# An attention stage beside a mixture layer on one core: q's transposes as fp32r from DMA copies, and the stages from the transposes on one slot later

## The chip, the cores and the metric

The kernel runs on one core of a Trainium2 chip. The metric is the device time of one execution in microseconds, the median of several runs. Engines are called as in the profile: PE (TensorE), DVE (VectorE), ACT (ScalarE), POOL (GpSimd) and SP (SyncE, which here only issues DMAs).

## What is computed

Three parts follow one another. The first is a linear attention with a complex decay per channel; the reference steps through the 768 positions of each of 4 x 8 heads of width 48:

```python
for t in range(S):
    ar, ai = (a_re_n[:, :, t, :, None], a_im_n[:, :, t, :, None])
    new_re = ar * S_re - ai * S_im
    new_im = ar * S_im + ai * S_re
    kv = np.einsum('bhd,bhe->bhde', k[:, :, t], v[:, :, t])
    S_re, S_im = (new_re + kv, new_im)
    y[:, :, t] = np.einsum('bhd,bhde->bhe', q[:, :, t], S_re)
```

Its result, 3072 tokens of 384, goes through `g = h * tanh(softplus(h))` with `h = x @ w_in` (384 to 2048) and `g @ w_out`, called the first layer here, and then through `(a * b) @ w_out` with `a = x @ w_a`, `b = x @ w_b` (384 to 1536), the second layer.

## The kernel before, in words

**Chunks.** The attention is cut into 24 chunks: six stretches of 128 positions for each of 4 batch entries, all 8 heads together. Chunk c belongs to stretch c // 4. In a chunk the decay's logarithm and its angle are summed along the positions by a product with a triangle matrix (`sum_ell`, `sum_theta`, line 329), exponentials and sines of the sums scale and rotate q and k (`scale_qk`, `trig`, `rotate`), and from there it is an ordinary masked attention with a running state: q and k are transposed on PE (line 410), four heads in one PSUM bank, so two banks for q and two for k; ACT copies them to SBUF (`qT`, `kT`); `scores` multiplies them (line 433) and DVE keeps the lower triangle in `am` (line 439); `values` adds the product of q with the state W and of the scores with v (line 463); `outer` and `state` bring W up to date (lines 502 and 515). `store_y` and `store_y2` split the result into a rounded part `yh` (ACT) and a rest `yl` (DVE), each in a tile of its own of which there is one, store both to DRAM, and `read_x` loads them as columns of the first layer's input `xh`, `xl`.

**Units.** The first layer works in 6 blocks of 512 tokens, one for each stretch, and 16 units of 128 hidden columns each. A unit is nine matmuls `hps` (line 594), a chain on DVE and ACT that ends in the product `m` (lines 600 to 614), its two parts `gh` and `gl` (lines 620, 621), and, two units later on PE, nine matmuls `x2ps` (line 637). In block 0 the product is not split, and `x2ps` takes three matmuls of plain float32. The second layer (lines 692 and 717) follows alone.

**Slots.** The first four chunks are worked before the first unit, in an order written out by hand. The other 20 run beside blocks 0 to 4, the four chunks of stretch j+1 beside block j. A table gives each step of a chunk a slot; chunks follow at 8 slots, and 32 slots go over a block's 16 units:

```python
early = [
    (-4, load_a), (0, decay_1), ..., (7, sum_theta), (6, decay_exp), (8, reduce_angle),
    (8, hand_turn), (7, hand_end), (7, scale_qk), (11, trig),
]
late = [
    (10, read_end), (11, load_v), (14, lambda c: transposes(c, 0)), (15, lambda c: transposes(c, 1)),
    (16, lambda c: scores(c, 0)), (16, lambda c: scores(c, 1)), (17, values), (17, outer),
    (17, state), (18, store_y), (19, store_y2), (20, read_x),
]
```

`load_qk` stands in slot 4 and `rotate` in slot 12. Where a block begins in slots is taken from the last entry of `late` (`ready_slot`, `ends`). A scheduler then sets the order on each engine from the written order, its own estimate of when things are ready, and the buffers: q, k, `qhp` (rotated q, in the tile QH) and `khp` have one buffer each, PSUM tiles of the tag `ps` three, and `hps` two. All DMAs of this part are issued by SP, in their order.

Of the kernel before, what the change touches and what calls it, by code (L numbers as in the profile page):

```python
# [10 lines left out]
F32 = mybir.dt.float32  # L11
F32R = mybir.dt.float32r
# [9 lines left out]
def kernel(  # L22
# [14 lines left out]
    nc = tc.nc  # L37
# [26 lines left out]
    B, H, S, D = q.shape  # L64
# [3 lines left out]
    P = 128  # L68
    C = 128
# [6 lines left out]
    HH = H // 2  # L76
# [13 lines left out]
    const = ctx.enter_context(tc.tile_pool(name="const", bufs=1))  # L90
    dram = ctx.enter_context(tc.tile_pool(name="dram", bufs=1, space=DRAM))

    ident = const.tile([P, P], F32, name="ident")
    csum = const.tile([P, P], F32, name="csum")
    csum_r = const.tile([P, P], F32R, name="csum_r")
    tsum = const.tile([P, P], F32, name="tsum")
    good_i = const.tile([1, 1], I32, name="good_i")
    bias_one = const.tile([P, 1], F32, name="bias_one")
# [27 lines left out]
    ap1 = att.enter_context(tc.tile_pool(name="ap1", bufs=1, side="right"))  # L126
# [5 lines left out]
    qT = [ap1.tile([P, HH, C], F32, name=f"qT{i}") for i in range(2)]  # L132
    W = [ap1.tile([P, H * D + PAD], F32, name=f"W{b}") for b in range(B)]
    QH, KH = (ap1.tile([P, 2 * H, 64], F32, name=nm) for nm in ("qhp", "khp"))
# [124 lines left out]
    def in_rows(c, nm):  # L259

        if c < B:
            return pair(c, nm, nm, "h", "a")
        own = QH if nm == "qh" else KH
        if nm == "qh":
            nc.gpsimd.memset(own[:, :, D:], 0.0)
        st[nm, c] = own.rearrange("p (h a) d -> p h a d", a=2)[..., :D]
        return st[nm, c]
# [124 lines left out]
    def rotate_one(c, nm, eng):  # L392
        w = st["turn", c].rearrange("p a h d -> p h a d")
        x = st.pop((nm, c)).rearrange("p h (o d) -> p h o d", o=1).to_broadcast([P, H, 2, D])
        eng.tensor_tensor(in_rows(c, nm + "h"), x, w, ALU.mult)

    def rotate(c):
        rotate_one(c, "q", nc.vector)
        rotate_one(c, "k", nc.vector)

    def transposed(c, nm, hf):

        src = st[nm[0] + "h", c]
        pool, tag = (ps_h, "h") if c < B and nm == "kT" else (ps_a, "ps")
        K = D2 if c < B else P
        p = pool.tile([P, HH, C], F32, tag=tag, name="p" + nm)[:K]
        own = (QH if nm == "qT" else KH).rearrange("p (h a) d -> p h (a d)", a=2)
        for i in range(HH):
            h = hf * HH + i
            nc.tensor.transpose(p[:, i, :], src[:, h].rearrange("p a d -> p (a d)") if c < B else own[:, h], ident)  # L410
        st["p" + nm, c, hf] = p

    def transposed_out(c, nm, hf):
        K = D2 if c < B else P
        if c % 2 and c < B:
            t = ap0.tile([P, HH, C], F32, tag=f"{nm}{hf}", name=nm)[:K]
        else:
            t = (qT[hf] if nm == "qT" else ap2.tile([P, HH, C], F32, tag=nm, name=nm))[:K]
        st[nm, c, hf] = t
        act(out=t, in_=st.pop(("p" + nm, c, hf)), func=AF.Copy)  # L420

    def transposes(c, hf):
        for nm in ("qT", "kT"):
            transposed(c, nm, hf)
            transposed_out(c, nm, hf)
# [4 lines left out]
    def scored_in(c, hf):  # L430
        p = st["psc", c, hf] = ps_a.tile([P, HH, C], F32, tag="ps", name="psc")
        for i in range(HH):
            nc.tensor.matmul(  # L433
                p[:, i, :], lhsT=st["kT", c, hf][:, i, :], rhs=st["qT", c, hf][:, i, :], start=True, stop=True
            )

    def scored_out(c, hf):
        causal = csum.bitcast(I32).rearrange("p (o c) -> p o c", o=1).to_broadcast([P, HH, C])
        nc.vector.copy_predicated(scored(c)[hf], causal, st.pop(("psc", c, hf)))

    def scores(c, hf):
        scored_in(c, hf)
        scored_out(c, hf)
# [103 lines left out]
    def slot_0(c):  # L547
# [3 lines left out]
    early = [  # L551
        (-4, load_a), (0, decay_1), (1, decay_2), (1, decay_3), (2, tangent), (2, decay_4), (3, angle),
        (3, split_ell),
        (4, carry), (4, split_theta), (5, sum_ell), (7, sum_theta), (6, decay_exp), (8, reduce_angle),
        (8, hand_turn), (7, hand_end), (7, scale_qk), (11, trig),
    ]
    late = [
        (10, read_end), (11, load_v), (14, lambda c: transposes(c, 0)), (15, lambda c: transposes(c, 1)),
        (16, lambda c: scores(c, 0)), (16, lambda c: scores(c, 1)), (17, values), (17, outer),
        (17, state), (18, store_y), (19, store_y2), (20, read_x),  # L560
    ]
    plan = {}
    for c in range(B, NCH):
        for n, (r, fn) in enumerate(early + late + [(4, load_qk), (12, rotate)]):
            plan.setdefault(slot_0(c) + r, []).append((-r, c, n, fn))
# [183 lines left out]
    def judge(pool):  # L749
# [20 lines left out]
        out=csum, in_=csum, pattern=[[1, P]], compare_op=ALU.is_ge, fill=0.0, base=0, channel_multiplier=-1  # L770
    )
    make_identity(nc, ident)
    nc.vector.tensor_copy(csum_r, csum)
    nc.vector.tensor_scalar(tsum, csum, 1.0 / TWO_PI, None, ALU.mult)
    for t in am + am0 + W + qT + [KH]:
        nc.gpsimd.memset(t, 0.0)
# [136 lines left out]
    for ui in range(len(units) + lag):  # L913
        if ui == 3:
            behind(after_lead, last)
        if ui < len(units):
# [6 lines left out]
            p = moe1_h(blk, f, ps_a if blk == NB - 1 and f % 2 else ps_h)  # L923
# [232 lines left out]
```

## Time and profile before

| | us |
|---|---|
| median of 3 runs | 1092.7 (1091.62 to 1093.75) |
| the profiled execution | 1092.23 |
| its span, first to last instruction | 1090.4 |
| PE busy | 1048.8 |
| DVE busy | 653.7 |
| ACT busy | 611.5 |
| POOL busy | 232.0 |

A busy time is the union of an engine's instructions. Matmuls overlap: one starts before the last has drained, so their mean durations add up to more than PE's busy time, and the spacing of two starts, not the duration, says what one costs in a full stream. In a row of a timeline "x4" merges four instructions of one kind; the time in it runs from the first start to the last end. Brackets at the end of a row hold the idle time before it and what ended it.

### The profile page before, as it was taken

Reading aid. Unit: us, or ns where it says so; the run is one execution under the profiler, and the core shown is the slowest. Engines: PE = TensorE matmul, PEld = TensorE weight load, DVE = VectorE, ACT = ScalarE, POOL = GpSimd, SP = SyncE. Lnnn points to the kernel's source line nnn. Section 1 sums busy time; section 2 is a strip of 40 time slices with the busy share of each in tenths; the row PEclk is TensorE's granted clock in tenths of the full one; section 3 lists DMA queues with packets and bytes.
Section 4 is the critical chain, followed back from the end, with each engine's and each line's share of the span. In section 5 each row is a group of like instructions: output and inputs, shape, how many; then the busy total and the mean of one; then the engine's idle time right before and its main releaser. Section 6 shows DMA issues by size and latency. Waiting matters only on the chain.

```text
span 1090.4 us, 15921 instructions
## 1 busy us (share of the span) xinstructions
PE 1048.8 (96%) x6060; PEld 874.0 (80%) x6060; DVE 653.7 (60%) x998; ACT 611.5 (56%) x968; POOL 232.0 (21%) x265
## 2 busy tenths in 40 slices
PE   4989999999999999999999999999999999999997
PEld 1856666788888888888877778888888888888886
DVE  6799966787677777777579998532322322422222
ACT  8868877898788887798767742221221222212211
POOL 2012343444334344333231123100000000000000
PEclk9989999999999999999999999999999999999999
DMA  9557752344434343433155366110100100100000
GB/s 206 107 153 191 173 152 66 67 96 87 111 80 82 67 95 80 87 97 80 30 164 183 124 217 212 43 58 1 30 29 1 58 1 1 44 1 1 29 1 32
DMA packets 203550, 90.92 MB, mean 83 GB/s; under 512 B 144782, under 2 KB 187851, under 8 KB 203467
## 3 DMA queue, kind: packets, MB, share of 16 engines
q1 hardware_dynamic: 202410, 89.62, 32.9%
q8 instruction: 50, 0.82, 0.3%
q10 hardware_dynamic: 1056, 0.21, 0.1%
q14 instruction: 34, 0.27, 0.1%
HBM read 72.44 MB, written 17.36 MB: 82 GB/s over the span
## 4 chain that ended last, share of the span: by engine, by line
PE 70%; DVE 13%; ACT 6%; issue 5%; DMA 3%; POOL 2%; SPq 1%; ACTq 0%; DVEq 0%; POOLq 0%
PE ops L717 12%; PE psb L692 12%; PE psa L692 12%; PE x2ps L637 12%; PE hps L594 11%; PE psc L433 3%; PE py L463 3%; ACT m L59 3%; PE pkT L410 2%; DVE wf L168 1%; PE pqT L410 1%; ACT L54 1%; DVE wf L169 1%; DVE m L600 1%; DVE wf L167 1%
## 5 line engine op out<-in xcount | busy, mean ns | idle before, releaser
L703 DVE TENSOR_TENSOR a_sb<-a_sb,psb 128x512 f32<-128x512 f32 x72 | 49.4, 686 | 224.9 <-PE psb L692 224.9
L59 ACT ACTIVATE m<-m 128x512 f32<-128x512 f32 x192 | 119.5, 632 | 68.8 <-DVE m L600 64.0
L59 ACT ACTIVATE a_sb<-psa 128x512 f32<-128x512 f32 x72 | 43.0, 597 | 163.6 <-PE psa L692 161.6
L59 ACT ACTIVATE ph<-a_sb 128x512 fp32r<-128x512 f32 x72 | 45.4, 631 | 155.5 <-DVE a_sb L703 155.5
L594 PE MATMUL hps<-xh,winh 128*128 128x512 f32 x288 | 119.1, 415 | 4.7 <-DVE gh L611 3.3
L621 POOL TENSOR_TENSOR gl<-m,gh 128x512 fp32r<-128x512 f32 x64 | 83.2, 1300 | 151.9 <-DVE gh L620 131.6
L594 PE MATMUL hps<-xh,winl 128*128 128x512 f32 x288 | 114.2, 396 | 0.0
L594 PE MATMUL hps<-xl,winh 128*128 128x512 f32 x288 | 114.1, 396 | 0.0
L717 PE MATMUL ops<-woh,ph 128*128 128x384 f32 x288 | 97.1, 337 | 0.0
L717 PE MATMUL ops<-woh,pl 128*128 128x384 f32 x288 | 97.1, 337 | 0.0
L717 PE MATMUL ops<-wol,ph 128*128 128x384 f32 x288 | 96.7, 336 | 0.0
L637 PE MATMUL x2ps<-gl,wouth 128*128 128x512 f32 x240 | 94.3, 393 | 2.4 <-DVE gl L621 1.4
L637 PE MATMUL x2ps<-gh,wouth 128*128 128x512 f32 x240 | 94.1, 405 | 1.8 <-ACT gh L59 1.5
L637 PE MATMUL x2ps<-gh,woutl 128*128 128x512 f32 x240 | 94.0, 392 | 0.0
L614 DVE SCALAR_TENSOR_TENSOR m<-m,hps 128x512 f32<-128x512 f32 x80 | 54.6, 684 | 63.1 <-ACT m L59 62.6
L692 PE MATMUL psa<-xh,wal 128*128 128x512 f32 x216 | 85.2, 394 | 0.0
L692 PE MATMUL psa<-xl,wah 128*128 128x512 f32 x216 | 85.1, 394 | 0.0
L692 PE MATMUL psa<-xh,wah 128*128 128x512 f32 x216 | 84.4, 391 | 0.3 <-DVE a_sb L703 0.3
L692 PE MATMUL psb<-xh,wbh 128*128 128x512 f32 x216 | 84.2, 390 | 0.0
L692 PE MATMUL psb<-xh,wbl 128*128 128x512 f32 x216 | 84.2, 390 | 0.0
L692 PE MATMUL psb<-xl,wbh 128*128 128x512 f32 x216 | 84.2, 390 | 0.0
L705 DVE TENSOR_TENSOR pl<-a_sb,ph 128x512 fp32r<-128x512 f32 x72 | 52.2, 726 | 39.0 <-ACT ph L59 39.0
(167 smaller groups left out, 2332.1 us busy)
## 6 DMA issues: line engine op xcount, KB each, us to landing
wraw<-in_moe_w_out_dram SPq DMA_DIRECT2D x14, 768.0 KB
wraw<-in_moe_w_in_dram SPq DMA_DIRECT2D x8, 768.0 KB
a<-in_a_re_dram SPq DMA_DIRECT2D x24, 192.0 KB
q<-in_q_dram SPq DMA_DIRECT2D x24, 192.0 KB
k<-in_k_dram SPq DMA_DIRECT2D x24, 192.0 KB
v<-in_v_dram SPq DMA_DIRECT2D x24, 192.0 KB
wraw<-in_moe_w_a_dram SPq DMA_DIRECT2D x6, 768.0 KB
wraw<-in_moe_w_b_dram SPq DMA_DIRECT2D x6, 768.0 KB
```

What stands on the lines that cost most here:

```text
L59: x = nc.scalar.activation(**kw)
L410: nc.tensor.transpose(p[:, i, :], src[:, h].rearrange("p a d -> p (a d)") if c < B else own[:, h], ident)
L433: nc.tensor.matmul(p[:, i, :], lhsT=st["kT", c, hf][:, i, :], rhs=st["qT", c, hf][:, i, :], start=True, stop=True)
L463: nc.tensor.matmul(p[par * 64:(par + 1) * 64, i, :], lhsT=w[:, col:col + 64], rhs=x[:, first + par, :], start=(n == 0), stop=(n == len(ter ...
L594: nc.tensor.matmul(p, lhsT=w[:, kk, :], rhs=x[:, kk, :], start=(i == 0), stop=(i == len(ops) - 1))
L614: nc.vector.scalar_tensor_tensor(m, m, 2.5, p, ALU.subtract, ALU.mult)
L621: (nc.vector if on_act else nc.gpsimd).tensor_tensor(gl, m, gh.bitcast(F32), ALU.subtract)
L637: nc.tensor.matmul(x2ps[m], lhsT=w[:, ms], rhs=x, start=(f == 0 and i == 0), stop=(f == NF - 1 and i == len(terms) - 1),)
L692: nc.tensor.matmul(p, lhsT=w[:, kk, :], rhs=x[:, kk, :], start=(i == 0), stop=(i == len(ops) - 1))
L703: nc.vector.tensor_tensor(a_sb, a_sb, pb, ALU.mult)
L705: nc.vector.tensor_tensor(lo, a_sb, hi.bitcast(F32), ALU.subtract)
L717: nc.tensor.matmul(ops_t[t], lhsT=x[:, tsl], rhs=w, start=(f == 0 and i == 0), stop=(f == NF2 - 1 and i == 2),)
```

## The change

q's transposes of the 20 later chunks take their operand from a copy of rotated q that two DMAs of 128 x 512 float32 (256 KB) write right behind the rotation, one for each half of the heads. The copies are typed fp32r, as are the identity and the view of PSUM that is written; bits are moved, none is rounded. The copies lie in the tiles `yh` and `yl`, taken under the same tags, so that a copy can be written once the previous chunk's result has been stored from there. k's transposes stay float32. In the table the transposes and all that follows stand one slot later, except `outer`, which stays in slot 17 and now stands ahead of `values`. `sum_theta`, `reduce_angle` and `hand_turn` stand one slot earlier. Blocks begin one slot later in slot numbers, so the later steps keep their distance to the units and the earlier ones come a slot sooner.

```diff
+    ident_r = const.tile([P, P], F32R, name="ident_r")
...
+    QR = []
+
     def rotate(c):
         rotate_one(c, "q", nc.vector)
+        QR[:] = [ap1.tile([P, HH, C], F32R, tag=nm, name="qr") for nm in ("yh", "yl")]
+        for hf in range(2):
+            nc.sync.dma_start(
+                out=QR[hf].bitcast(F32), in_=QH[:, hf * H:(hf + 1) * H].rearrange("p (h a) d -> p h (a d)", a=2)
+            )
         rotate_one(c, "k", nc.vector)
...
             h = hf * HH + i
+            if c >= B and nm == "qT":
+                nc.tensor.transpose(p[:, i, :].bitcast(F32R), QR[hf][:, i], ident_r)
+                continue
             nc.tensor.transpose(p[:, i, :], src[:, h].rearrange("p a d -> p (a d)") if c < B else own[:, h], ident)
...
-        (4, carry), (4, split_theta), (5, sum_ell), (7, sum_theta), (6, decay_exp), (8, reduce_angle),
-        (8, hand_turn), (7, hand_end), (7, scale_qk), (11, trig),
+        (4, carry), (4, split_theta), (5, sum_ell), (6, sum_theta), (6, decay_exp), (7, reduce_angle),
+        (7, hand_turn), (7, hand_end), (7, scale_qk), (11, trig),
     ]
     late = [
-        (10, read_end), (11, load_v), (14, lambda c: transposes(c, 0)), (15, lambda c: transposes(c, 1)),
-        (16, lambda c: scores(c, 0)), (16, lambda c: scores(c, 1)), (17, values), (17, outer),
-        (17, state), (18, store_y), (19, store_y2), (20, read_x),
+        (10, read_end), (11, load_v), (15, lambda c: transposes(c, 0)), (16, lambda c: transposes(c, 1)),
+        (17, lambda c: scores(c, 0)), (17, lambda c: scores(c, 1)), (17, outer), (18, values),
+        (18, state), (19, store_y), (20, store_y2), (21, read_x),
     ]
...
+    nc.vector.tensor_copy(ident_r, ident)
```

Three places show what the scheduler makes of it; all are of chunk 15, beside block 2. `hps`, `gh` and `m` are the units' tiles, `pt` the angle sums, `pqT` and `pkT` the transposed banks.

On PE before, from the last `hps` matmul of a unit through the chunk's transposes:

```order
930 L594 MATMUL hps<-xh,winl_1303 128x512
931 L410 MATMUL pqT<-ident,qhp 128x128 x4
932 L410 MATMUL pkT<-ident,khp 128x128 x4
933 L637 MATMUL x2ps_2980<-gh,wouth_2340 128x512
...
942 L410 MATMUL pqT<-ident,qhp 128x128 x4
943 L410 MATMUL pkT<-ident,khp 128x128 x4
944 L329 MATMUL pt<-sh,csum_r 128x384
```

and after the change:

```order
919 L330 MATMUL pt<-sh,csum_r 128x384
...
929 L605 MATMUL hps<-xh,winl_1319 128x512
930 L419 MATMUL pqT<-ident_r,qr 128x128 x4
931 L421 MATMUL pkT<-ident,khp 128x128 x4
932 L648 MATMUL x2ps_3030<-gh,wouth_2375 128x512
...
941 L419 MATMUL pqT<-ident_r,qr 128x128 x4
942 L421 MATMUL pkT<-ident,khp 128x128 x4
```

The transposes stand behind the same unit as before, and the angle sums have moved from behind them to a unit ahead.

On DVE before, around the rotation of q (`qhp<-q,a`) and k (`khp<-k,a`):

```order
418 L614 SCALAR_TENSOR_TENSOR m<-m,hps 128x512
419 L600 TENSOR_SCALAR m<-hps 128x512
420 L620 CAST gh<-m 128x512
421 L395 TENSOR_TENSOR qhp<-q,a 128x16x48
422 L395 TENSOR_TENSOR khp<-k,a 128x16x48
423 L307 SCALAR_TENSOR_TENSOR a<-size,a 1x384
```

and after the change:

```order
415 L319 TENSOR_TENSOR sl<-size,sh 128x384
416 L526 TENSOR_TENSOR W_132<-W_132,pu 128x384
417 L396 TENSOR_TENSOR qhp<-q,a 128x16x48
418 L495 TENSOR_TENSOR yl<-py,yh 128x512
419 L611 TENSOR_SCALAR m<-hps 128x512
420 L396 TENSOR_TENSOR khp<-k,a 128x16x48
```

The rotation stands one unit of the first layer earlier (on ACT, its sines too), directly ahead of the previous chunk's `yl` and of the first step of the next unit's chain, `m<-hps`.

On SP before, the DMA issues from v's load to the next chunk's `a`:

```order
199 L237 DMA v<-in_v_dram 128x8x48
200 L534 DMA xh<-yt_dh_74 128x3x128
201 L534 DMA xl<-yt_dl_75 128x3x128
202 L218 DMA q<-in_q_dram 128x8x48
203 L218 DMA k<-in_k_dram 128x8x48
204 L218 DMA a<-in_a_re_dram 128x8x48
205 L218 DMA a<-in_a_im_dram 128x8x48
```

and after the change:

```order
208 L498 DMA yt_dh_75<-yh 48x4x128 x2
209 L498 DMA yt_dl_76<-yl 48x4x128 x2
210 L219 DMA q<-in_q_dram 128x8x48
211 L404 DMA qr<-qhp 128x512 x2
212 L219 DMA k<-in_k_dram 128x8x48
213 L219 DMA a<-in_a_re_dram 128x8x48
214 L219 DMA a<-in_a_im_dram 128x8x48
215 L545 DMA xh<-yt_dh_75 128x3x128
216 L545 DMA xl<-yt_dl_76 128x3x128
```

The copies `qr` stand behind the stores of `yh` and `yl`, whose tiles they fill, and behind the next load of q; the loads of `xh` and `xl` have moved behind them and behind k and `a`.

## Rows read from the trace of the kernel before

**Rows 1.** The page, busy time of each engine over the span.

```profile
PE 1048.8 (96%) x6060; PEld 874.0 (80%) x6060; DVE 653.7 (60%) x998; ACT 611.5 (56%) x968; POOL 232.0 (21%) x265
```

**Rows 2.** Busy us of each engine in four stretches, then clock, DMA share, GB/s.

```profile
60.00:90.00 30.00, 25.60 (x122) 17.14 (x119) 28.75 (x46) 22.01 (x36) 4.52 (x5) 0.89 0.62 177
...
90.00:120.00 30.00, 29.30 (x229) 20.77 (x229) 29.51 (x43) 24.45 (x37) 7.76 (x8) 1.00 0.76 190
...
120.00:150.00 30.00, 27.98 (x166) 18.93 (x165) 27.89 (x35) 25.07 (x38) 18.41 (x14) 1.00 0.60 154
...
180.00:570.00 390.00, 383.99 (x2633) 321.54 (x2632) 286.01 (x455) 319.27 (x507) 155.52 (x181) 1.00 0.39 86
```

**Rows 3.** Groups by shape: busy us, mean ns of one, idle before.

```profile
L410 PE MATMUL pqT<-ident,qhp 128*128 128x128 f32 x160 | 24.2, 273 | 2.2 <-DVE qhp L395 2.2
...
L433 PE MATMUL psc<-qT,kT 128*128 128x128 f32 x320 | 39.5, 276 | 2.7 <-ACT wouth L59 1.3 <-ACT kT L59 0.7 <-ACT qT L59 0.7
...
L637 PE MATMUL x2ps<-gh,wout 128*128 128x512 f32 x96 | 43.8, 594 | 0.0
...
L594 PE MATMUL hps<-xh,winl 128*128 128x512 f32 x288 | 114.2, 396 | 0.0
...
L410 PEld LDWEIGHTS pqT<-ident,qhp 128*128 128x128 f32 x160 | 19.4, 140 | 10.5 <-issue 3.3 <-POOL gl L621 1.6 <-DVE qhp L395 0.9
...
L433 PEld LDWEIGHTS psc<-qT,kT 128*128 128x128 f32 x320 | 38.8, 191 | 4.8 <-ACT wouth L59 1.5 <-ACT qT L59 1.1 <-ACT kT L59 0.9
...
L773 DVE CAST csum_r<-csum 128x128 fp32r<-128x128 f32 x1 | 0.2, 220 | 0.0
```

**Rows 4.** TensorE in order of time, 348 to 372 us: start us, us, then the work.

```profile
348.21 0.60 PE L410 MATMUL pqT<-ident,qhp 128*128 128x128 f32 x4
...
351.35 0.60 PE L410 MATMUL pqT<-ident,qhp 128*128 128x128 f32 x4
...
351.78 0.60 PE L410 MATMUL pkT<-ident,khp 128*128 128x128 f32 x4
...
370.17 0.39 PE L594 MATMUL hps<-xh,winh 128*128 128x512 f32 x1
```

**Rows 5.** What TensorE waited for: us in total, times, longest us.

```profile
PE pqT L410 <- DVE qhp L395: 2.2, 3, 1.2
...
PE pkT L410 <- DVE khp L395: 1.0, 3, 0.5
...
PE py L463 <- DVE am L439: 0.7, 1, 0.7
```

**Rows 6.** VectorE in order of time, 346 to 372 us.

```profile
346.31 1.48 DVE L395 TENSOR_TENSOR qhp<-q,a 128x768 f32<-128x768 f32 x1 [0.72 <-ACT a L59]
...
361.33 0.69 DVE L484 TENSOR_TENSOR yl<-py,yh 128x512 fp32r<-128x512 f32 x1 [0.80 <-ACT yh L59]
...
367.99 0.69 DVE L614 SCALAR_TENSOR_TENSOR m<-m,hps 128x512 f32<-128x512 f32 x1 [2.27 <-ACT m L59]
...
370.33 1.47 DVE L395 TENSOR_TENSOR qhp<-q,a 128x768 f32<-128x768 f32 x1 [0.73 <-ACT a L59]
```

**Rows 7.** ScalarE in order of time, 343 to 386 us.

```profile
345.25 0.53 ACT L59 ACTIVATE a<-a 128x384 f32<-128x384 f32 x1
...
345.68 0.60 ACT L59 ACTIVATE a<-a,bias_hpi 128x384 f32<-128x384 f32 x1
...
384.58 0.60 ACT L59 ACTIVATE x2o<-x2ps 128x512 f32<-128x512 f32 x1 [0.86 <-DMA x_d<-x2o]
```

**Rows 8.** SyncE (its DMA issues) in order of time, 345 to 384 us.

```profile
347.82 0.37 SPq L218 DMA_DIRECT2D q<-in_q_dram  x1
...
362.21 0.93 SPq L487 DMA_DIRECT2D yt_dl<-yl  x2
...
364.89 0.36 SPq L534 DMA_DIRECT2D xl<-yt_dl  x1
...
382.47 1.76 SPq L648 DMA_DIRECT2D x_d<-x2o  x2
```

## The prediction

> **What bounds the kernel.** I read the busy times first: PE is busy for 96% of the span [rows 1]. Matmuls overlap, so a busy PE need not be a full one; the stretches tell more [rows 2]. From 180 to 570 us, where 16 of the 20 later chunks run beside blocks 1 to 4, PE is busy for 383.99 of 390 us and DVE for 286.01: what PE saves there comes off the end, as long as nobody else becomes late. From 60 to 150 us, where the first four of the 20 run beside block 0, DVE is busy for 28.75, 29.51 and 27.89 of 30 us: there PE's gain is worth little. The waits of PE [rows 5] say what its idle time hangs on near the transposes. Last I read four queues in order of time: PE [rows 4], DVE [rows 6], ACT [rows 7], SP [rows 8].
>
> **Part 1: q's transposes.** Four transposes take 0.60 us from the first start to the last end [rows 4], one lasts 273 ns [rows 3]: three spacings share 0.33 us, so one costs 109 ns in the stream. What sets that? A float32 matmul of 128 columns that is not a transpose lasts 276 ns, the same [rows 3], so a transpose streams like float32. In fp32r 512 columns last 396 ns, in float32 594 [rows 3]: 198 ns less, or 0.39 ns a column, 50 ns for 128. The other limit is the load of the stationary operand. In the scores it lasts 191 ns, in the transposes 140 for as many columns [rows 3]: 51 ns shorter. If the load keeps this shortness in fp32r, the stream sets the pace, and a transpose costs 109 - 50, about 60 ns.
>
> The Trainium skill ("TensorE: Matmul & The Clock Gate", section "LDWEIGHTS (loading the stationary operand)") has a rule against this: a load takes P / 1.2 ns for P columns, 107 ns here, whatever the number of columns that stream. By it the load would set a pace of 107 ns, and the gain would be nothing. The two kinds of load in rows 3 differ by 51 ns at equal columns, which the rule does not have.
>
> The trace of before has no fp32r transpose, so the gain lies between 0 (the load or the transpose itself keeps 109 ns) and 50 ns each. I take 50, because the row nearest to it, the float32 transpose, has the short load. That is 8 x 50 ns, 0.40 us a chunk: 6.4 us over 16 chunks. For the four chunks beside block 0 I count nothing, with a bound of 1.6 us.
>
> **Part 2: one slot between rotation and transposes.** Before, the rotation of q waits for the sines (0.72 us, [rows 6]), begins at 346.31, ends at 347.79, and PE begins to transpose at 348.21 [rows 4], 0.42 us later. In the waits of PE, transposes stood 2.2 us for q and 1.0 us for k, and the values 0.7 us for the masked scores [rows 5], 3.9 us in all. The change puts the rotation one unit ahead of where it was, and the values a slot behind the scores. Two rotations are 24.02 us apart [rows 6], so a slot is 3.0 us and a unit 6.0. These waits should go; I take 3.0 us of the 3.9, since some stood beside block 0, where the next wait, for DVE's decoding, is close behind.
>
> **Part 3: the copies.** Each chunk gets two DMAs of 256 KB. Behind the end of the rotation SP issues the load of q (0.37 us, [rows 8]), then the two copies. The nearest transfer is the store of `x2o`, as large and with the same rows of 2 KB: issued at 382.47, it released ACT at 384.58 [rows 7, 8], 2.1 us. So the first copy should land about 2.9 us after the rotation, some 3.6 if it waits for the bytes of q in front. The second waits besides for `yl`, which now follows the rotation on DVE: 0.69 us, then its stores, which before took from 362.21 to the dependent load at 364.89 [rows 8], 2.7 us, then 2.4 for the copy: 5.8 us. PE needs the first 6.4 us after the rotation (0.42 and a unit of 6.0), the second 3.1 us later (348.21 to 351.35, [rows 4]). Spare time: 2.8 us and 3.7. If the rotation came only one slot earlier, 3.4 us, the first copy would be 0.2 late. I count nothing, with a bound of 1 us a chunk beside block 0, where the queue also carries weights (DMA share 0.62 to 0.76, [rows 2]): 4 us.
>
> The bytes themselves, 0.5 MB a chunk, lie beside a DMA share of 0.39 [rows 2] and cost nothing. The copy of the identity is one more DVE instruction like that of the triangle, 0.22 us [rows 3], beside the first loads: nothing, at most 0.2. Moving `outer` ahead of `values` fills PE while DVE masks; the angle sums and `reduce_angle` come earlier and nobody waits for them: nothing.
>
> **Part 4: what comes later.** SP issues in order, so the loads of `xh` and `xl` now stand behind q, two copies, k and two of `a`, six issues of some 0.4 us, and behind the 2.7 us of `yl`'s stores. Only the last chunk of a block is awaited: before, its `xl` was issued at 364.89 and the next block began at 370.17 [rows 4, 8], 5.3 us, of which the transfer takes about 2.7 like the store. Spare are 2.6 us; the new order takes `yl` behind sines and rotation (about 2 us) and the loads 3.4 us further back, but moves a set of transposes and nine `x2ps` ahead of the block's first matmul. I take 0.5 us at each of three boundaries, 1.5 us, between 0 and 4.5.
>
> **Sum.** The profiled execution took 1092.2 us, 0.5 below the median. 1092.2 - 6.4 - 3.0 + 1.5 = 1084.3 us; against the median that is -0.8%. About 0.2%, 2.2 us, is what a measurement of this kernel can tell from no change.
>
> **Rivals.**
>
> *The transposes get no faster.* The load of 128 columns, or the transpose's own path, keeps 109 ns. For it: a load of 191 ns [rows 3] is as usual for fp32r weights as for float32, and the trace has no short load in fp32r. Against it: the short load goes with transposing. Time: 1092.2 - 3.0 + 1.5 = 1090.7, no change within the bound. This is what the Trainium skill's rule for loads, above, amounts to. Chance 0.22.
>
> *The unit's chain comes late* (slower). DVE is a queue: `m<-hps` now stands behind the rotation and `yl`, which wait for ACT's sines, a table load and `yh`; ACT takes both before the next unit's exponential. `hps` has two buffers, so two units later PE waits for the product `m<-m,hps`. Before, that product ended at 368.68 [rows 6] and the matmul that needs its buffer began at 370.17 [rows 4]: 1.5 us to spare. It decides from 1.5 us of added delay on; each 0.5 us beyond, over 16 chunks, takes back 8 us, all that the forecast gains. At 1.0 us beyond: 1084.3 + 16 = 1100.3. For it: the rotation already waits for the sines in rows 6. Against it: the sines move a unit earlier too, and ACT is busy for 319.27 of 390 us [rows 2]. Chance 0.12.
>
> *The copies land late* (slower). If the rotation stays close to the transposes, as before, PE waits for the DMA: at 0.42 us instead of 6.4 the first copy would be 3 us late; with half of that for 16 chunks, 24 us, the time is 1108. It outweighs the gain from 0.5 us late a chunk on. Against it: the DVE order above. Chance 0.08.
>
> **How the numbers follow.** The forecast has 0.58. Its own range begins at 1079.5 (1092.2 - 6.4 - 1.6 - 3.9 = 1080.3 with block 0's gain, all the waits and no loss at boundaries, and 0.8 for waits not listed) and ends at 1089 (a loss of 4.5 instead of 1.5 at boundaries, and 1.7 of the copies' bound of 4). With the first rival the range is 1079.5 to 1093.0, which leaves out the slower two. Faster by over 0.2%: nearly all of the forecast (0.56), 0.09 of the first rival: 0.65. Slower: 0.12 + 0.08, less 0.04 for mild cases: 0.16, and 0.02 of the first rival: 0.18. No change: 0.17.
>
> **What would show it.** Right: fp32r transposes spaced 60 ns, four in some 0.4 us; loads of about 140 ns; no wait of PE for `qhp`, `khp` or the copies; DVE's rotation ending about 6 us before the transposes; the stretch of blocks 1 to 4 shorter by some 8 us. Wrong: transposes still at 109 ns; a wait of PE on a DMA into `qr`; `hps` waiting for DVE's `m`; a gap at the start of a block, ended by the load of `xh` or `xl`.

## The result, and the profile after

The change makes the kernel slower: 1100.86 us (median of 5 runs, 1098.69 to 1102.46) against 1092.27 of the kernel before (5 runs, 1090.72 to 1093.75), a ratio of 1.0073 with a 95% interval of 1.0061 to 1.0084. That is 8.0 us more; forecast were 8.4 us less, and the range ended at 1093.0. The profiled execution took 1098.69 us, the fastest of the five, with a span of 1097.0.

Below, and in the experiments, a step's worth in us is a difference of two such ratios times 1092, since the medians of the kernel before, which was run again with each group of experiments, differ by up to 1.3 us (1090.97 to 1092.27).

The stretches of [rows 2], now of the kernel after (busy us of PE, PE's loads, DVE, ACT and POOL, then clock, DMA share, GB/s):

```profile
60.00:90.00 30.00, 23.69 (x166) 15.69 (x162) 30.00 (x46) 22.34 (x36) 5.95 (x5) 1.00 0.66 190
90.00:120.00 30.00, 29.12 (x224) 20.00 (x224) 27.84 (x43) 25.94 (x41) 5.79 (x8) 1.00 0.70 192
120.00:150.00 30.00, 28.98 (x170) 19.76 (x170) 27.39 (x34) 23.72 (x36) 18.80 (x14) 1.00 0.70 179
...
180.00:570.00 390.00, 380.60 (x2605) 313.67 (x2604) 271.85 (x441) 315.84 (x495) 153.71 (x176) 1.00 0.45 104
```

From 180 to 570 us PE is idle for 9.4 us, before for 6.0. What it waited for, against [rows 5], in the whole span of the kernel after:

```profile
...
PE hps L605 <- DVE gh L622: 4.1, 4, 1.6
PE pkT L421 <- ACT qT L59: 3.6, 3, 3.0
PE pt L330 <- POOL sh L317: 2.7, 3, 1.9
PE pqT L419 <- DMA qr<-qhp: 2.3, 4, 0.9
PE pqT L419 <- DVE a L355: 1.8, 3, 0.9
PE hps L605 <- DVE m L625: 1.5, 3, 0.9
...
PE pt L330 <- DVE sl L321: 1.4, 4, 0.7
```

The three waits of [rows 5] are gone, as forecast. In their place stand the angle sums `pt`, which wait for the two parts `sh` and `sl` of the angle; `pqT`, which waits for the copies and for `reduce_angle` (line 355), whose end frees the PSUM bank of the angle sums; and `pkT`, which waits for ACT to empty the bank of `pqT` (3.0 of its 3.6 us in one place of block 0, where four banks are wanted within 5 us and there are three).

Where the time went is told best by the starts of the units. PE's first matmul of units 0, 17, 40 and 80, in order of time, in the kernel before:

```profile
52.50 0.50 PE L594 MATMUL hps<-xh,winh 128*128 128x512 f32 x1
...
175.26 0.39 PE L594 MATMUL hps<-xh,winh 128*128 128x512 f32 x1
...
322.12 0.39 PE L594 MATMUL hps<-xh,winh 128*128 128x512 f32 x1
...
557.66 0.39 PE L594 MATMUL hps<-xh,winh 128*128 128x512 f32 x1
```

and in the kernel after:

```profile
53.09 0.50 PE L605 MATMUL hps<-xh,winh 128*128 128x512 f32 x1
...
177.91 0.39 PE L605 MATMUL hps<-xh,winl 128*128 128x512 f32 x1
...
329.19 0.39 PE L605 MATMUL hps<-xh,winh 128*128 128x512 f32 x1
...
565.27 0.39 PE L605 MATMUL hps<-xh,winh 128*128 128x512 f32 x1
```

Between them PE does the same work in both kernels, but for a few instructions. I call the stretches A (units 0 to 17: block 0), B (17 to 40: block 1 and half of block 2) and C (40 to 80: ten chunks). They take 122.8, 146.9 and 235.5 us before, and 124.8, 151.3 and 236.1 after: +2.0, +4.4 and +0.5. Ahead of unit 0 it is +0.6, behind unit 80 it is -1.1, as in most of the traces. So the change loses beside blocks 0 to 2, and in C, where gain was expected most, it is even. This table, read in the same way from every trace, is what the experiments are weighed by. Each trace is one execution, and executions of one kernel differ (the five of the change by 3.8 us), so a us or two in one stretch proves nothing.

| kernel | ratio to before, 95% | A | B | C |
|---|---|---|---|---|
| the change | 1.0073 (1.0061 to 1.0084) | +2.0 | +4.4 | +0.5 |
| e1 angle sums back | 1.0070 (1.0056 to 1.0084) | +2.6 | +6.5 | +0.4 |
| e2 angle sums alone | 1.0113 (1.0098 to 1.0129) | +3.4 | +2.8 | +7.5 |
| e3 slots, float32 | 1.0110 (1.0094 to 1.0125) | +1.2 | +5.5 | +4.6 |
| e4 fp32r, old slots | 1.0117 (1.0102 to 1.0133) | +1.4 | -0.4 | +9.1 |
| e5 later slots alone | 1.0243 (1.0230 to 1.0256) | +4.4 | +8.1 | +14.1 |
| e6 outer behind values | 1.0038 (1.0025 to 1.0051) | -1.3 | +5.0 | +0.3 |
| e7 k's sets first | 1.0028 (1.0018 to 1.0037) | -1.7 | +1.3 | +3.3 |
| e8 q's second half | 0.9987 (0.9978 to 0.9996) | -0.6 | +1.0 | -0.7 |
| e9 angle sums behind | 1.0147 (1.0124 to 1.0170) | +5.6 | +9.1 | +0.1 |
| e10 k rotated first | 1.0030 (1.0018 to 1.0043) | -1.9 | +0.6 | +4.6 |
| e11 second `sh` | 1.0082 (1.0068 to 1.0096) | +4.2 | +5.6 | +0.9 |
| e12 `sh`, `outer`, `r` | 1.0071 (1.0057 to 1.0084) | +1.9 | +3.9 | +3.2 |
| e13 `sl` on POOL | 1.0104 (1.0087 to 1.0121) | +2.1 | +9.2 | -0.7 |
| e14 the same, `outer` | 1.0080 (1.0066 to 1.0094) | +2.5 | +8.6 | -1.2 |
| e15 q's and k's half | 1.0066 (1.0052 to 1.0079) | -1.8 | +1.4 | +6.5 |
| e16 outer first alone | 1.0095 (1.0080 to 1.0111) | -1.6 | +1.3 | +8.9 |
| e17 copies, float32 | 1.0114 (1.0098 to 1.0129) | +4.2 | +5.9 | +1.7 |
| e18 half copy, float32 | 1.0000 (0.9991 to 1.0009) | -1.6 | +0.3 | +0.6 |

TensorE's granted clock stands in these numbers too. Before, it is 0.97 over A (0.89 from 60 to 90 us, [rows 2]); in the change it is 1.00 over A, B and C, so its +2.0 in A is rather too small. Over B it is 1.00 before, in the change and in e3, but 0.99 in e1, e2, e5, e6, e9, e11, e12, e13 and e17 and 0.98 in e14; over C it falls below 1.00 in e5 alone. A place of B in e1, PE and then a stretch with columns as in [rows 2]:

```profile
306.11 0.59 PE L605 MATMUL hps<-xh,winh 128*128 128x512 f32 x1 [0.73 <-DVE m L625]
...
306.40:310.00 3.60, 3.60 (x10) 2.79 (x10) 1.37 (x3) 1.41 (x3) 3.41 (x3) 0.53 0.78 152
```

PE had stood 1.20 us for a copy and 0.73 us for a product; then the clock was near the lower of its two levels (1.2 against 2.4 GHz), and matmuls `hps` started 0.43 us apart instead of 0.23. Over the nine of this unit that is some 1.6 us (an estimate from these spacings), most of the 2.1 by which e1's B exceeds the change's.

### The profile page after: what moved, and what is told of

Its sections match the earlier page's. It is cut to its first block, busy times and chain, and to the rows that moved or that the text cites. A ratio compares the mean times of both kernels' runs of the same rounds, so it can differ in the third digit from the quotient of the medians.

```text
span 1097.0 us, 15985 instructions
## 1 busy us (share of the span) xinstructions
PE 1050.1 (96%) x6060; PEld 869.6 (79%) x6060; DVE 647.0 (59%) x999; ACT 615.5 (56%) x968; POOL 237.1 (22%) x265
## 4 chain that ended last, share of the span: by engine, by line
PE 48%; DVE 7%; ACT 4%; DMA 2%; issue 2%; POOL 1%; POOLq 0%; ACTq 0%; SPq 0%; DVEq 0%
PE ops L728 13%; PE psa L703 13%; PE psb L703 13%; PE x2ps L648 4%; PE hps L605 3%; ACT m L59 3%; DVE m L611 1%; DVE m L625 1%; DMA good_d<-good 1%; DMA k<-in_k_dram 1%; PE py L474 1%; DVE wf L169 0%; PE psc L444 0%; DVE qhp L396 0%; POOL gl L632 0%
## 5 line engine op out<-in xcount | busy, mean ns | idle before, releaser
L632 POOL TENSOR_TENSOR gl<-m,gh 128x512 fp32r<-128x512 f32 x64 | 86.2, 1347 | 109.1 <-DVE gh L631 93.0
L611 DVE TENSOR_SCALAR m<-hps 128x512 f32<-128x512 f32 x96 | 65.5, 683 | 20.5 <-PE hps L605 15.0
```

Of the source, the lines that this page charges most:

```text
L611: nc.vector.tensor_scalar(m, p, 20.0, None, ALU.min)
L632: (nc.vector if on_act else nc.gpsimd).tensor_tensor(gl, m, gh.bitcast(F32), ALU.subtract)
```

## The experiments

### The parts of the change, one by one (e1 to e4)

The first reading blamed the angle sums: their waits are the most visible new ones. e1 is the change with them back:

```diff
-(6, sum_theta), (7, reduce_angle), (7, hand_turn)
+(7, sum_theta), (8, reduce_angle), (8, hand_turn)
```

> The change with one part undone: the angle sums, reduce_angle and the hand turn are back in their old slots, behind the first half of the transposes. Theory (the angle sums, now in front of the transposes, make PE wait for the split of theta and hold a PSUM bank until reduce_angle): 4 to 6 us of the loss in blocks 1 to 3 go, and some of block 0's 1.6; about 1095 us against 1100.9 for the change; PE's waits of the angle sums on sh and sl (2.7 and 1.4 us) and of pqT on reduce_angle (1.8 us) are gone. Rival (the copies or their traffic): no angle sums involved, stays at 1100 to 1101. Rival (outer ahead of values costs PE time in every chunk): stays at 1099 to 1101.

Measured: 1099.13 us, ratio 1.0070, no difference from the change. The waits of `pt` for `sh` and `sl` are gone, but in B transposes wait for ACT (2.1 us) and for copies (2.8 us) instead. The first theory fell here.

e2 is the kernel before with the same three entries moved forward, and nothing else:

```diff
-(7, sum_theta), (8, reduce_angle), (8, hand_turn)
+(6, sum_theta), (7, reduce_angle), (7, hand_turn)
```

> The kernel before with one part of the change alone: angle sums, reduce_angle and hand turn one slot earlier; no copies, float32 transposes, all else where it was. Theory (angle sums): slower by 3 to 6 us, 1095 to 1098, with PE waiting for sh and sl at the angle sums. Rival (copies, outer ahead of values, or the later slot of the transposes): within 1 us of 1092.3.

Measured: 1103.88 us, ratio 1.0113, 12 us slower, though not by the wait that was expected. In C `pt` waits for ACT, which has still to read the sums of the sizes from one of the three PSUM banks (PE's waits, 330 to 562 us of e2):

```profile
PE pt L329 <- ACT size L59: 4.1, 9, 0.7
```

e3 is the change without copies, q's transposes again in float32 from the rows:

```diff
-        QR[:] = [ap1.tile([P, HH, C], F32R, tag=nm, name="qr") for nm in ("yh", "yl")]
-        for hf in range(2):
-            nc.sync.dma_start(
-                out=QR[hf].bitcast(F32), in_=QH[:, hf * H:(hf + 1) * H].rearrange("p (h a) d -> p h (a d)", a=2)
-            )
...
-                nc.tensor.transpose(p[:, i, :].bitcast(F32R), QR[hf][:, i], ident_r)
```

> The change's whole order without the copies: q's transposes are float32 again and read q's rotated rows directly. Theory (angle sums): the loss stays, and the 25 ns that fp32r saves on each of some 128 transposes beside blocks 1 to 4 come on top, 3.2 us: 1102 to 1104. Rival (copies: traffic on the DMA queues, or SP's issues standing in front of the loads): 1092 to 1096, since nothing is copied.

Measured: 1102.71 us, ratio 1.0110: the order of the change alone costs 12.0 us, and copies and fp32r together give 4.0 back. The rival about the copies falls.

e4 has copies and fp32r with both tables of before; of the second the first row stands for all:

```diff
-(6, sum_theta), (7, reduce_angle), (7, hand_turn)
+(7, sum_theta), (8, reduce_angle), (8, hand_turn)
-        (15, lambda c: transposes(c, 0)), (16, lambda c: transposes(c, 1)),
+        (14, lambda c: transposes(c, 0)), (15, lambda c: transposes(c, 1)),
```

> The copies and fp32r transposes in the old order: transposes one slot after the rotation, as before, so that the copies have next to no time. Theory: PE waits 2.4 to 3.5 us a chunk for the first copy where nothing else covers it, 16 to 20 chunks, less 3.2 us for the faster transposes: 1128 to 1158 if the rotation ends 0.42 us ahead of the transposes as before. If copies land early enough even so: 1089, and the later slot was not needed. The wait of PE for qr gives the time that a copy takes from the end of the rotation.

Measured: 1103.51 us, far less bad than expected. PE waits 15.2 us for `qr`, 15 times, at most 1.4. A place in C of e4 (DVE's rotation, SP's two issues, PE's transposes):

```profile
347.66 1.47 DVE L396 TENSOR_TENSOR qhp<-q,a 128x768 f32<-128x768 f32 x1 [0.73 <-ACT a L59]
...
349.19 1.12 SPq L404 DMA_DIRECT2D qr<-qhp  x2
...
351.63 0.51 PE L419 MATMUL pqT<-ident_r,qr 128*128 128x128 f32 x4 [1.08 <-DMA qr<-qhp]
```

The rotation ends at 349.13 and PE begins at 351.63: a copy takes 2.5 us from the end of the rotation, with SP's issue right behind it. PE was ready only 1.1 us too early, because the scheduler had put four `x2ps` in front; the expectation had taken the 0.42 us of [rows 4]. The later slot is needed for the copies, then, but it is worth about 1.0 us in each of 15 chunks and not 3.

### The later slots alone (e5), and outer (e6, e16)

e5 is the kernel before with the change's table `late`: float32 transposes, no copies, angle sums where they were.

```diff
-        (14, lambda c: transposes(c, 0)), (15, lambda c: transposes(c, 1)),
-        (16, lambda c: scores(c, 0)), (16, lambda c: scores(c, 1)), (17, values), (17, outer),
-        (17, state), (18, store_y), (19, store_y2), (20, read_x),
+        (15, lambda c: transposes(c, 0)), (16, lambda c: transposes(c, 1)),
+        (17, lambda c: scores(c, 0)), (17, lambda c: scores(c, 1)), (17, outer), (18, values),
+        (18, state), (19, store_y), (20, store_y2), (21, read_x),
```

> The kernel before with the later slots alone: transposes, scores, outer, values, state and stores as in the change; float32 transposes without copies, angle sums where they were. Theory after the first four runs (the new order costs, the transposes gain): the change less fp32r's gain, which the first four traces put at 4.5 to 5 us from 174 to 565 us, so slower than before by 9 to 13 us, 1100 to 1104. Rival (the later slots are harmless; the loss of the run with the angle sums back came from the copies): 1091 to 1094.

Measured: 1118.34 us, ratio 1.0243: 26.5 us slower, twice what was expected. Earlier angle sums take 14.5 of that back (e5 to e3), copies and fp32r 18.9 (e5 to e1). The parts do not add up one by one: each repairs some of what the later slots break. One thing that they break is the order in DVE's queue. In C, DVE in order of time:

```profile
457.88 2.05 DVE L395 TENSOR_TENSOR qhp<-q,a 128x768 f32<-128x768 f32 x1
459.86 0.54 DVE L515 TENSOR_TENSOR W<-W,pu 128x384 f32<-128x384 f32 x1
460.32 0.95 DVE L395 TENSOR_TENSOR khp<-k,a 128x768 f32<-128x768 f32 x1
461.19 0.68 DVE L484 TENSOR_TENSOR yl<-py,yh 128x512 fp32r<-128x512 f32 x1
461.79 0.68 DVE L600 TENSOR_SCALAR m<-hps 128x512 f32<-128x512 f32 x1
...
465.40 0.69 DVE L614 SCALAR_TENSOR_TENSOR m<-m,hps 128x512 f32<-128x512 f32 x1 [2.47 <-ACT m L59]
```

and PE, which had finished that unit's `hps` (the last of nine), and then waits for the product that frees their buffer; the last row is a stretch right behind, with columns as in [rows 2]:

```profile
457.38 0.39 PE L594 MATMUL hps<-xh,winl 128*128 128x512 f32 x1
...
466.14 0.50 PE L594 MATMUL hps<-xh,winh 128*128 128x512 f32 x1 [1.87 <-DVE m L614]
...
467.00:470.40 3.40, 3.40 (x12) 2.74 (x11) 1.87 (x4) 2.09 (x4) 2.25 (x2) 0.50 0.59 132
```

The unit's matmuls end at 457.77; its first DVE step `m<-hps` starts at 461.79, 4.0 us later, because both rotations, the state and `yl` stand in front of it in DVE's queue. I worked out this lateness for all units (start of `m<-hps` less end of the unit's last `hps`, none counted below zero): in C 0.60 us on the mean before, 1.57 in e5; in B 0.54 before and 1.03 in the change. A part of e5's loss is the clock's: behind this wait it is 0.50 for 3.4 us, and in C also from 388.5 to 395.2, some 10 us at half speed in all, which can have cost some 5 of the 14.1 us at most.

e6 is the change with `outer` behind `values` again. `outer` there reads rows of `khp` over which the sizes of the chunk after next have been written, so the state gets other numbers; the work is the same.

```diff
-(17, outer), (18, values),
+(18, values), (18, outer),
```

> The change with outer behind values again, both in slot 18. Theory: outer between scores and the next half of a set costs PE 0.28 us a chunk in the trace of the change (two more passages from one kind of matmul to another), so some 4 us of 16 to 20 chunks come back: 1096 to 1097. Rival (the order of outer does not matter, waits elsewhere take the time): 1100 to 1101.

Measured: 1095.57 us, ratio 1.0038: 3.8 us of the loss gone. The size was right and the place wrong: nearly all of it lies in A (-1.3 instead of +2.0, the clock 1.00 in both), next to none in C. B, at +5.0, hides what it may have gained, since the clock there is 0.99. Two causes stay mixed here, since e6 also frees the sizes from waiting for `outer`.

e16 moves `outer` alone in the kernel before, one slot earlier, behind the scores:

```diff
-(16, lambda c: scores(c, 1)), (17, values), (17, outer),
+(16, lambda c: scores(c, 1)), (16, outer), (17, values),
```

> The kernel before with outer alone one slot earlier, behind the scores and ahead of values, as in the change. Theory (two more passages on PE, 0.25 to 0.3 us a chunk): slower by 3 to 5 us, 1094.5 to 1096.5. Rival (its cost belongs to the later slots): within 1 us of before, or faster, since khp is free earlier.

Measured: 1101.49 us, ratio 1.0095, twice the expected cost. PE then waits for the rotated rows in C (2.8 us for q's, 1.9 for k's), and `m<-hps` is late by 1.49 us on the mean: it fits DVE's queue again, more than the passages on PE.

### The angle sums again (e9, e11 to e14)

e9 puts the angle sums behind the second half of the transposes, as they stood before relative to them:

```diff
-(6, sum_theta), (7, reduce_angle), (7, hand_turn)
+(8, sum_theta), (9, reduce_angle), (9, hand_turn)
```

> The change with the angle sums two slots later and reduce_angle and hand_turn with them, so that they stand behind the second half of the transposes, where they stand in the kernel before relative to the transposes. Theory (the two parts of theta use the same buffers sh and sl as those of ell; they can be written only behind PE's sums of ell, and the change left 2.4 us between the two sums where 6.5 were, while POOL, DVE and the queue between them need 2.7): waits of pt for sh and sl go, and no set of transposes waits for a bank held by the angle sums: 4 to 6 us less than the change, 1095 to 1097. Rival (the loss comes from r, which waits for khp until outer has read it): stays at 1099 to 1101.

Measured: 1106.38 us, ratio 1.0147, 8 us worse than the change, all in A and B; C stays even. With `reduce_angle` later the sines and the rotation are later too, and PE waits 8.8 us for `qr`, up to 4.0 at once. So the change needs its angle sums early: sines, rotation, copy and transposes are one chain.

e11 keeps the change's order and gives `sh` a second buffer, so that the high part of the angle need not wait for the size sums `pl`.

```diff
-tag="s" + i, name="s" + i) for i in "hl")
+tag="s" + i, name="s" + i, bufs=2 if i == "h" else 1) for i in "hl")
```

> The change's order, with a second buffer for the high part (sh) alone; the room comes from keeping the identity and the triangle once instead of twice. POOL can then write theta's high part ahead of the sums of ell; only sl still waits for them. Theory: the waits of pt for sh (2.7 us) go and those for sl shrink: 2 to 4 us less than the change, 1097 to 1099. Rival (sh and sl are late because the size calculation is late): no difference, 1100 to 1101.

Measured: 1100.61 us, ratio 1.0082, no gain. One place in C shows why (POOL, PE and DVE):

```profile
426.58 0.51 POOL L316 TENSOR_SCALAR sh<-a 128x384 fp32r<-128x384 f32 x1 [1.84 <-ACT m L59]
...
427.04 0.34 PE L329 MATMUL pl<-sh,csum_r 128*128 128x384 f32 x1
...
428.03 0.69 DVE L624 SCALAR_TENSOR_TENSOR m<-m,hps 128x512 f32<-128x512 f32 x1 [1.61 <-ACT m L59]
428.63 0.68 DVE L610 TENSOR_SCALAR m<-hps 128x512 f32<-128x512 f32 x1
...
429.23 0.75 DVE L320 SCALAR_TENSOR_TENSOR sl<-a,sh 128x384 fp32r<-128x384 f32 x1
...
430.04 0.44 PE L329 MATMUL pt<-sl,csum_r 128*128 128x384 f32 x1 [0.24 <-DVE sl L320]
```

`sh` is now early, but `sl` stands on DVE behind the unit's product, which waits for ACT's last exponential.

e12 adds `outer` behind `values` to e11, with `r` out of `khp` so that `outer` reads whole rows:

```diff
+            act(out=spare, in_=s[:, 1], func=AF.Exp, scale=-0.5)
+            act(out=s[:, 0], in_=s[:, 0], func=AF.Exp, scale=-0.5)
```

> The second buffer for sh, outer behind values, and r no longer in khp: its two halves go in place into the squares and into the free half of a, with one more ACT instruction a chunk, so that outer reads whole rows and the size calculation does not wait for it. Theory: 4 to 5 us less for the order of outer and 2 to 4 for sh: 1091 to 1094, and no wait of DVE's tangent product for khp. Rival (something else in the later slots costs): 1095 or more.

Measured: 1099.45 us, ratio 1.0071. e6's gain is not there; `pt` waits 5.3 us for `sl`.

e13 is e11 with the low part of the angle on POOL, and e14 is e12 with the same:

```diff
+            nc.gpsimd.tensor_scalar(x, x, scale, 0.0, ALU.mult, ALU.add)
...
-            nc.vector.scalar_tensor_tensor(lo, x, scale, hi.bitcast(F32), ALU.mult, ALU.subtract)
+            nc.gpsimd.tensor_tensor(lo, x, hi.bitcast(F32), ALU.subtract)
```

> The change's order with the second sh and theta's low part on POOL instead of DVE, where it stood behind the unit's product, which waits for ACT's last exponential. Theory (the waits of the angle sums come from DVE's queue): waits of pt for sl and sh go, 4 to 5 us in the stretch from 174 to 565 us, and the time falls by 3 to 5 us, 1096 to 1098. Rival (what PE saves at the angle sums is lost at the next wait, since the unit's chain over ACT and DVE sets the pace there): the waits of pt go, hps or the transposes wait instead, 1099 to 1101.

> The same with outer behind values and r outside khp. Theory: 4 to 5 us less than the run with both freed, 1094 to 1096. Rival (as above): 1098 to 1100.

Measured: 1101.71 us (1.0104) and 1100.34 us (1.0080). In C both are the fastest of the later-slot kernels (-0.7 and -1.2 to before), so there the theory about DVE's queue fits, for 1.2 and 1.7 us against the change, read from one execution each; in B POOL's three steps are later still, and `pt` waits there instead (for POOL 7.7 us in e13, 4.3 in e14; B loses 9.2 and 8.6 us). Neither expectation for the whole came true.

### What fp32r is worth (e7, e8, e10, e15, e17, e18)

These keep the order of before, or change nothing but the kind of transpose. e7 and e10 take the change's copies and fp32r transposes of q into the old slots, and transpose both halves of k in slot 14 and of q in slot 15; e10 rotates k first as well (the last two rows):

```diff
-(14, lambda c: transposes(c, 0)), (15, lambda c: transposes(c, 1)),
+(14, lambda c: transposes(c, "kT")), (15, lambda c: transposes(c, "qT")),
...
+        rotate_one(c, "k", nc.vector)
         rotate_one(c, "q", nc.vector)
```

> Copies and fp32r transposes in the old slots, but k's two sets in the first slot of the transposes and q's two in the second, so that a copy has 3 us more; angle sums and all behind as before. Theory (fp32r gains about 0.2 us a bank of four, and only order and late copies take it back): no wait for qr, 8 x 50 ns in each of 16 chunks: 1086 to 1088. Rival (copies cost by their traffic or by SP's issues in front of the loads, or the pace of the transposes gives nothing): 1091 or more.

> The run with k's sets in the first slot, with k now rotated ahead of q. There PE waited 0.6 to 1.2 us in each chunk for k's rotation, 9 us in all. Theory: these waits go, q's copies start 0.95 us later and still have 2 to 3 us: 1086 to 1088.5. Rival (copies then late): a wait for qr of 0.5 us or more in each chunk, 1091 or more.

Measured: 1094.46 us (1.0028) and 1095.15 us (1.0030). In e7 PE waits for k's rotation, in e10 for the copies, as PE's waits from 175 to 565 us say, of e7 and of e10:

```profile
PE pkT L421 <- DVE khp L396: 9.1, 13, 1.4
```

```profile
PE pqT L419 <- DMA qr<-qhp: 4.2, 14, 0.5
```

e8 copies and transposes only q's second half in fp32r, in the old slots; e15 also k's second half (`kr`):

```diff
-            if c >= B and nm == "qT":
+            if c >= B and nm == "qT" and hf:
...
+            if c >= B and hf:
```

> Only q's second half copied and transposed in fp32r, in the old slots; the first half stays float32 and reads the rows directly. PE's order is that of before. Theory: the copy has 3 us more than in the run in the old slots, no wait, half the gain: 1089 to 1090. Rival (fp32r gains nothing, or copies cost): 1092 or more.

> The kernel before with the second half of q and the second half of k copied and transposed in fp32r, all slots as before. Theory (fp32r gains 0.2 us a bank of four where the order stays): two banks a chunk, 16 chunks, less what the run with q's half alone already showed (0.7 us): 1088 to 1090. Rival (k's copy, which starts 0.95 us later, is late): PE waits for kr, 1091 or more.

Measured: e8 1090.70 us, ratio 0.9987 (0.9978 to 0.9996), the only one below the kernel before; the gain of 1.4 us is real by its interval but under the 0.2% that the prediction called telling. e15 1098.24 us (1.0066): PE waits 8.2 us for k's copy, 14 times, at most 1.2.

e17 is the change with its copies, transposed in float32; e18 is e8 in the same manner:

```diff
-nc.tensor.transpose(p[:, i, :].bitcast(F32R), QR[hf][:, i], ident_r)
+nc.tensor.transpose(p[:, i, :], QR[hf].bitcast(F32)[:, i], ident)
```

> The change with q's transposes in float32, read from the copies as before from the rows; all slots as in the change. Theory (the gain is fp32r's, 0.2 us a bank of four): about 0.4 us a chunk slower than the change beside blocks 2 to 4, where PE sets the pace, 4 us, and less beside blocks 0 and 1: 1104 to 1106. Rival (the gain of the change over the same slots without copies came from q's rows being free earlier): as the change, 1100 to 1101.

> The run with q's second half copied, transposed in float32 from the copy. Theory: slower than that run by 0.2 us a chunk beside blocks 2 to 4, about 2 us: 1092 to 1093.5. Rival (fp32r is worth nothing here): 1090 to 1091.

Measured: e17 1103.32 us (1.0114), e18 1091.30 us (1.0000). So fp32r gives 4.5 us in the change, with some 2 us of uncertainty, and 1.4 us for half of the banks in the order of before, where the intervals of e8 and e18 overlap, so that the uncertainty is as large as the gain; the copies by themselves give nothing in the whole (e3 to e17: 1.0110 to 1.0114), though in C they take back 2.9 us, which fits q's rows being free earlier, though no run shows that.

Two banks of the change and two of e17, PE in order of time:

```profile
452.83 0.46 PE L419 MATMUL pqT<-ident_r,qr 128*128 128x128 f32 x4
453.13 0.62 PE L421 MATMUL pkT<-ident,khp 128*128 128x128 f32 x4
```

```profile
456.79 0.60 PE L419 MATMUL pqT<-ident,qr 128*128 128x128 f32 x4
457.22 0.60 PE L421 MATMUL pkT<-ident,khp 128*128 128x128 f32 x4
```

A bank of q's takes 0.30 us to the start of k's, in float32 0.43. Over all twenty such banks of C the four starts are 70, 70, 70 and 84 ns apart, in float32 109 each: 142 ns a bank, 35 a transpose. Against the kernel before there is more, too short for the lists of waits: k's first transpose started there 203 ns behind q's last one on the mean of these banks, now 84. With both, q's banks of C take 5.9 us instead of 10.6. That C is even all the same means that the rest of the new order loses some 5 us there.

## Why the prediction was wrong, by its steps

**Part 1 held in kind and was mis-sized.** The transposes do get faster, by 35 ns each and not 50: the pace is 73 ns on the mean, not 60. By that the 16 chunks give 8 x 35 ns x 16 = 4.5 us instead of 6.4, and the pair of the change and e17 agrees (4.5, with some 2 us of uncertainty). The loads answer to [rows 3]; columns as there:

```profile
L419 PEld LDWEIGHTS pqT<-ident_r,qr 128*128 128x128 f32 x160 | 17.3, 140 | 12.6 <-issue 3.7 <-DVE a L355 2.9 <-DMA qr<-qhp 1.8
```

```profile
L419 PE MATMUL pqT<-ident_r,qr 128*128 128x128 f32 x160 | 20.3, 250 | 4.2 <-DMA qr<-qhp 2.3 <-DVE a L355 1.8
```

A load keeps its 140 ns, as assumed from the float32 transpose. The rival that the transposes get no faster is refuted: transposes, each with a load of its own, followed one another at 70 to 84 ns. The rule of the Trainium skill ("TensorE: Matmul & The Clock Gate", "LDWEIGHTS (loading the stationary operand)") gives 107 ns for a load of 128 columns; the pace of 107 ns that the prediction drew from it is not what this trace shows, and neither is the duration, 140 ns here and 191 in the scores [rows 3].

**Part 2 is the step that failed.** "These waits should go; I take 3.0 us of the 3.9": they went, but the later slots, with the order that they bring, cost 12.0 us (e3). In its sum the prediction priced the slot on PE alone, by the waits that it removes; what it does to DVE's queue stood only in a rival. On DVE the same slot puts rotations, state and `yl` of one chunk in front of `m<-hps` of a unit. A place of B in the kernel after, DVE and PE:

```profile
253.27 1.58 DVE L396 TENSOR_TENSOR qhp<-q,a 128x768 f32<-128x768 f32 x1
...
254.77 0.68 DVE L495 TENSOR_TENSOR yl<-py,yh 128x512 fp32r<-128x512 f32 x1
255.37 0.94 DVE L396 TENSOR_TENSOR khp<-k,a 128x768 f32<-128x768 f32 x1
...
256.71 0.67 DVE L611 TENSOR_SCALAR m<-hps 128x512 f32<-128x512 f32 x1
...
260.78 0.69 DVE L625 SCALAR_TENSOR_TENSOR m<-m,hps 128x512 f32<-128x512 f32 x1 [1.32 <-ACT m L59]
...
261.39 0.55 DVE L355 TENSOR_TENSOR a<-pt,a 128x384 f32<-128x384 f32 x1
```

```profile
253.41 0.39 PE L605 MATMUL hps<-xh,winl 128*128 128x512 f32 x1
...
261.99 0.54 PE L419 MATMUL pqT<-ident_r,qr 128*128 128x128 f32 x4 [0.23 <-DVE a L355]
```

The unit's matmuls end at 253.80, `m<-hps` starts 2.9 us later, the product ends at 261.47, and behind it stands `reduce_angle`, for whose PSUM bank the next transposes wait; PE loses 0.23 us at this place. The order on DVE is that of the rival "the unit's chain comes late", which had a chance of 0.12 and gave 1100.3 us; measured are 1100.9. That the two agree is luck: the rival put the loss at `hps`, in all 16 chunks of blocks 1 to 4, but PE's waits of `hps` for `m` are 1.5 us in all, before 1.4, and ten of these chunks, in C, lose next to nothing on balance. PE lost the time at `pt`, `pqT` and `pkT` and beside blocks 0 to 2.

**"The angle sums and `reduce_angle` come earlier and nobody waits for them: nothing"** was wrong as it stands: PE itself waits, 2.7 us for `sh` and 1.4 for `sl`. Yet putting them back gains nothing (e1), and given the later slots the sums are better early (e9, and e5 to e3). The trap was to read a wait that replaced another as a loss that could be undone.

**"Moving `outer` ahead of `values` fills PE": nothing** was wrong by 3.8 us, as far as e6 shows, which changes PE's order and frees `khp` at once.

**Part 3 held, though its first copy was mis-timed.** It put q's load alone in front of the first copy, and `yl`'s stores in front of the second. SP issues both copies behind these stores; a place of C in the kernel after:

```profile
442.44 1.60 DVE L396 TENSOR_TENSOR qhp<-q,a 128x768 f32<-128x768 f32 x1
...
444.66 0.79 SPq L498 DMA_DIRECT2D yt_dl<-yl  x2
...
446.12 1.52 SPq L404 DMA_DIRECT2D qr<-qhp  x2
```

Here the copies' issue begins 2.1 us behind the rotation's end; with the 2.5 us of e4 the first is ready about 4.5 us behind it (an estimate) and not 2.9. In C the transposes follow 6.4 to 9.7 us behind the rotation, and PE waits for no copy; ahead of C it is 3.7 to 7.5 us, and PE waits for `qr` 2.3 us in all, four times. The bound was 4 us. The rival "copies land late" came true in the old slots, at 1.0 us a chunk (e4), and with later angle sums (8.8 us, e9).

**Part 4**, 1.5 us at the boundaries, was not what happened: no wait of PE for `xh` or `xl` is in the trace of the kernel after.

The sum is then -4.5 (fp32r), +12.0 (order) and +0.4 (copies, e3 to e17): +7.9, where 8.0 were measured, since the terms are differences of the same runs, and -7.9 (-6.4 - 3.0 + 1.5) forecast.

**Open.** Why the later slots cost 3.9 to 9.2 us in B, in every kernel that has them (the change, e1, e3, e5, e6, e9, e11 to e14, e17), and less than 3 in every one that has not, is argued from DVE's queue and shown at single places, not by a run: no kernel was made that puts `m<-hps` ahead of the rotations there. e12 to e14 took away single waits of PE, and the time came back at others. In B the lateness of `m<-hps` is 0.79 to 1.14 us in these eleven traces and 0.49 to 0.75 in the rest, but it does not follow the loss: e14 has 0.79 and loses 8.6 us, the change 1.03 and 4.4; in C e14 has 1.12 and gains 1.2. Nor do waits say all: those of PE in B add up to 6.3 us after and 4.0 before, 2.3 of the 4.4. The passages that `outer` ahead of `values` adds, 0.28 us in each of B's six chunks by e6's expectation, may be 1.7 more, and in nine of the eleven the lower clock has a share. Beside that, e6's gain in A stays split between PE's order and the freed `khp`.

## What to carry to other kernels

Where a static order is tight, price a moved step on every in-order queue that it passes, not on the engine whose waits it removes: which instruction of the main chain now stands behind it, and what is waiting for that. Look at when buffers come free as well, since steps that seem independent may be tied by one buffer (here `sh` and `sl`, three PSUM banks, the rows of q and k). A faster instruction is best tried where nothing else moves: half of this gain, in the old order (e8), beat the whole change by 9 us.

## What was not expected of the hardware

An fp32r transpose of 128 columns costs 70 ns behind another one and 84 ns in front of a float32 transpose (means of C), against 109 in float32, though its load lasts 140 ns in both and its matmul 250 instead of 277 ns (the change and e17): spacing, and neither duration, gave the price. And the place of a matmul group has a price of its own: behind the last score the first `x2ps` starts 31 ns later (16 cases from unit 17 on, before), the first `pu` 205 ns later (12 cases, after).
